# Squares of three blocks taken head by head with ScalarE's accumulator, k and v of two batches on 96 partitions, and a new order of the queues

## Chip, core and metric

One core of a Trainium2 chip. The engines are TensorE (PE; its weight loads PEld), VectorE (DVE), ScalarE (ACT), GpSimd (POOL) and SyncE (SP), whose queue issues nearly all DMAs. The metric is the device time of one launch in microseconds, the median of the runs.

## What is computed

Three layers in a row on 4 batches of 576 tokens (2304 tokens, 8 heads of 64): linear attention with an RMS norm per head, a layer with Mish, and a layer with SoLU and a layer norm. All inputs are float32.

```python
kv = einsum('bhsd,bhse->bhde', k, v)              # 64 x 64 for each batch and head
o = einsum('bhsd,bhde->bhse', q, kv)
x = o / sqrt(mean(o * o, -1) + 1e-6) * g_norm     # per token and head
h = x @ w_in                                      # 512 -> 2048
y = (h * tanh(softplus(h))) @ w_out               # 2048 -> 512
z = y @ w2_in                                     # 512 -> 1024
s = z * softmax(z)
out = (s - mean(s)) / sqrt(var(s) + 1e-6) * g_ln @ w2_out
```

## The kernel before

**Tiles.** The tokens are cut into six blocks of 384 (three units of 128: block b, unit r). Blocks 0, 1, 3, 5 are the first 384 tokens of batches 0 to 3; blocks 2 and 4 hold the last 192 tokens of two batches each. Large matmuls run in fp16 with hi and lo parts (three passes), so every weight is decoded first: a piece of 128x1024 words is loaded (`ld`), scaled on ACT (`sc`, L598), signed on POOL (`sg`, L603), put together on DVE (`low` L608, `put` L615) and split into fp16 hi on ACT (`whi`, L626) and lo on DVE (`wlo`, L633 and L635). Pieces ("1", f) are w_in, ("2", f) are w_out.

**Attention.** `ld(b,i)` loads k and v of a pair of heads (`load_pair`, L340 to L350). For batches 0 and 1 (`WIDE`) two heads share 128 partitions, 64 each, in nine rows. For batches 2 and 3 a head's first 512 tokens lie on 128 partitions in four rows, and its last 64 tokens come with `ldr(b)` (`load_rest`, L333 to L338), four DMAs per batch in runs of 256 bytes. `kv(b,i)` (`kv_pair`, L365 to L380) makes one pair's products as fp32 matmuls of 64 columns, two per step, one for each head; the trace has two records for each. `kvf`, `kvg` and `kvh`, `kvl` bring the products into SBUF, on ACT and DVE. For each unit of blocks 0 and 1 then run: `qf`, `qT` (PE), `qc` (ACT, L447), `xo` (PE, o = q times kv, into a PSUM bank), `sq` (ACT: square of all eight heads, 128x512, L497), `ms` (DVE: sum per head, L502), `ep` and `rho` (POOL: add 1e-6, power -1/2, L506 and L512), `xf` (DVE, L518), `xP` (PE), `xhi` (ACT, L466), `xlo` (DVE, L471). Units of blocks 2 to 5 go another way for q and x (`qhi`, `qlo`, DMA transposes) but have the same `xo`, `sq`, `ms`, `ep`, `rho`, `xf`. Blocks 0 to 2 square straight from the PSUM bank; blocks 3 to 5 copy to SBUF first (`xc`).

**Mish layer.** `H0(i,r)` (block 0, first group, in parts of 128 tokens) and `H(b,g,i)` (384 tokens, 12 matmuls) make h in one of three PSUM banks, which `mi(b,g,i)` (ACT, L877) frees; `ghi` (ACT, L884) and `glo` (DVE, L889) split the result, and `Y(b,g,j)` multiplies by w_out. From `Hp(1,2,1)` on the products take a form with seven instead of eight multiplications. The last layer follows.

**Order.** Every operation is a task with an engine, a cost and its predecessors. SEQUENCE is a list of task numbers, found beforehand; tasks are issued in this order, and each engine runs its own in that order, one behind the other. `plan.timed` only gives the times by which `keep_warm` (L1704) fills expected gaps of PE with unused matmuls.

Of the kernel before, what the change touches and what calls it, by code (L numbers as in the profile page):

```python
# [7 lines left out]
FP32 = mybir.dt.float32  # L8
FP16 = mybir.dt.float16
I32 = mybir.dt.int32  # L10
ACTF = mybir.ActivationFunctionType
# [1756 lines left out]
```

## Time and profile before

| | |
|---|---|
| median of 3 runs | 579.49 us (579.33 to 579.74) |
| the profiled execution | 579.91 us |
| its span, first to last instruction | 578.1 us |
| PE busy | 571.4 us (99%) |
| DVE busy | 441.2 us (76%) |
| ACT busy | 367.4 us (64%) |
| POOL busy | 129.3 us (22%) |
| granted TensorE clock, mean | 0.999 |

Times in rows are microseconds from the start of the span. A start and a duration of one row and the start of the next on the same engine tell how long the engine was held: on ACT the next instruction often starts before the last has ended. The busy shares are means over stages with different limits; the first 60 us look unlike the rest.

### The profile page before, as it was taken

The numbers are of one execution on the slowest core, as the hardware profiler recorded it, in microseconds if no ns is written. First come the engines' busy times: TensorE is split into PE (matmuls) and PEld (weight loads), VectorE is DVE, ScalarE is ACT, GpSimd is POOL, SyncE is SP. The second block draws the span as 40 slices with busy tenths as digits, with TensorE's granted clock in tenths as the row PEclk, the third lists the DMA queues.
The fourth block names the chain that finished last, engine by engine and source line by source line (L and its number), as shares of the span: only waits on it lengthen the run. The fifth ranks groups of instructions, "written<-read, shape, count | busy, mean of one in ns | idle before, by whom it ended". The sixth has DMA issues, their size and how long they took to land.

```text
span 578.1 us, 12245 instructions
## 1 busy us (share of the span) xinstructions
PE 571.4 (99%) x4920; PEld 413.8 (72%) x4920; DVE 441.2 (76%) x745; ACT 367.4 (64%) x636; POOL 129.3 (22%) x185
## 2 busy tenths in 40 slices
PE   8999999999999999999999999999999999999997
PEld 7886666666678877887777787774545557677886
DVE  2899898899958978787573876996575998697851
ACT  2688666675737643364645567774769797888841
POOL 1766422331022301101100101000305305234300
PEclk9999999999999999999999999999999999999999
DMA  8996979928505380225114232281056448676995
GB/s 317 367 237 169 250 207 323 238 84 177 80 1 75 38 248 12 69 93 177 62 73 157 82 128 84 83 289 48 1 137 183 91 74 164 130 163 135 219 221 155
DMA packets 132090, 84.42 MB, mean 146 GB/s; under 512 B 96450, under 2 KB 119362, under 8 KB 131778
## 3 DMA queue, kind: packets, MB, share of 16 engines
q1 hardware_dynamic: 131888, 83.58, 56.7%
q8 instruction: 38, 0.62, 0.4%
q14 instruction: 18, 0.15, 0.1%
q10 hardware_dynamic: 146, 0.07, 0.0%
HBM read 46.67 MB, written 12.06 MB: 102 GB/s over the span
## 4 chain that ended last, share of the span: by engine, by line
PE 96%; DMA 2%; SPq 0%; issue 0%; DVE 0%; ACT 0%; POOL 0%; POOLq 0%; DVEq 0%
PE y L907 33%; PE hp L833 19%; PE h L1016 14%; PE op L1162 13%; PE hp L739 11%; PE kvp L379 2%; PE xo L481 2%; DMA yT<-in_v_dram 1%; DMA w<-ws 1%; PE hp L1707 1%; PE xo L453 1%; PE xTp L461 0%; PE qTp L441 0%; SPq L346 0%; DVE kvf L384 0%
## 5 line engine op out<-in xcount | busy, mean ns | idle before, releaser
L907 PE MATMUL y<-g,w 128*128 128x384 f16 x1152 | 202.5, 326 | 0.0
L907 PEld LDWEIGHTS <-w 128*128 128x128 f16 x1152 | 110.7, 98 | 66.9
L603 POOL TENSOR_SCALAR st<-st 128x512 f32<-128x512 f32 x48 | 41.0, 858 | 211.0 <-ACT P L598 201.0
L1162 PEld LDWEIGHTS <-w 128*128 128x128 f16 x768 | 74.1, 98 | 12.8 <-DMA w<-ws 0.6
L1162 PE MATMUL op<-yT,w 128*128 128x256 f16 (+1 forms) x576 | 72.4, 271 | 0.4 <-DMA w<-ws 0.4
L889 DVE SCALAR_TENSOR_TENSOR g<-m,g 128x768 f16<-128x768 f32 x48 | 45.8, 961 | 15.4 <-ACT g L884 15.1
L739 PEld LDWEIGHTS <-w 128*128 128x128 f16 x480 | 41.2, 98 | 21.3
L833 PEld LDWEIGHTS <-w 128*128 128x128 f16 x576 | 48.4, 98 | 3.7
L833 PEld LDWEIGHTS <-ws 128*128 128x128 f16 x576 | 48.5, 98 | 3.4
L739 PE MATMUL hp<-xT,w 128*128 128x384 f16 (+1 forms) x384 | 49.8, 286 | 0.0
L608 DVE SCALAR_TENSOR_TENSOR st<-st 128x512 int32<-128x512 int32 x48 | 33.5, 706 | 13.7 <-POOL st L603 13.6
L598 ACT ACTIVATE P<-st 128x512 f32<-128x512 f32 x48 | 32.1, 671 | 16.1 <-DMA st<-in_moe_w_in_dram 7.8
L1071 POOL TENSOR_SCALAR small<-small 128x1 f32<-128x1 f32 x18 | 13.0, 720 | 131.6 <-ACT e L1053 131.2
L884 ACT ACTIVATE g<-m 128x768 f16<-128x768 f32 x48 | 39.9, 838 | 3.7 <-PE y L907 3.5
L1016 PEld LDWEIGHTS <-w 128*128 128x128 f16 x210 | 20.6, 98 | 22.3
L1016 PE MATMUL h<-st,w 128*128 128x512 f16 x150 | 35.0, 379 | 0.0
L615 DVE SCALAR_TENSOR_TENSOR P<-P,st 128x512 int32<-128x512 int32 x48 | 33.1, 703 | 1.0
L512 POOL TENSOR_TENSOR rho<-ms,nhalf 128x8 f32<-128x8 f32 x18 | 31.0, 1727 | 1.0
L1162 PE MATMUL op<-ws,w 128*128 128x256 f16 (+1 forms) x192 | 31.1, 271 | 0.0
L850 ACT ACTIVATE st<-hp 128x384 f32<-128x384 f32 x32 | 15.5, 485 | 24.2 <-PE hp L833 24.2
L833 PE MATMUL hp<-xT,ws 128*128 128x192 f16 x336 | 30.8, 246 | 0.0
L1016 PEld LDWEIGHTS <-ws 128*128 128x128 f16 x168 | 16.4, 98 | 17.7
(164 smaller groups left out, 1007.0 us busy)
## 6 DMA issues: line engine op xcount, KB each, us to landing
st<-in_moe_w_in_dram SPq DMA_DIRECT2D x24, 512.0 KB, 6.1
st<-in_moe_w_out_dram SPq DMA_DIRECT2D x24, 512.0 KB, 5.1
w_far<-F SPq DMA_DIRECT2D x15, 256.0 KB, 2.4
qraw<-in_q_dram SPq DMA_DIRECT2D x4, 768.0 KB, 6.2
w_far<-st SPq DMA_DIRECT2D x11, 256.0 KB, 2.6
out_dram<-yT SPq DMA_DIRECT2D x11, 256.0 KB, 2.4
yT<-w_far SPq DMA_DIRECT2D x3, 896.0 KB, 4.9
st<-w_far SPq DMA_DIRECT2D x5, 512.0 KB, 7.1
```

The costliest lines, as they stand in the source:

```text
L512: nc.gpsimd.tensor_tensor(out=rho, in0=ms, in1=nhalf, op=ALU.pow)
L598: nc.scalar.activation(out=P, in_=v[:, :, 1], func=ACTF.Copy, scale=2.0 ** -111)
L603: nc.gpsimd.tensor_scalar(out=v[:, :, 1], in0=v[:, :, 1], scalar1=0.0, scalar2=1.0, op0=ALU.mult, op1=ALU.mult)
L608: nc.vector.scalar_tensor_tensor(out=v[:, :, 0], in0=v[:, :, 0], scalar=29, in1=v[:, :, 1], op0=ALU.logical_shift_right, op1=ALU.bitwise_or)
L615: nc.vector.scalar_tensor_tensor(out=P.bitcast(I32), in0=P.bitcast(I32), scalar=3, in1=v[:, :, 0], op0=ALU.logical_shift_left, op1=ALU.bit ...
L739: nc.tensor.matmul(out=h_t[b, grp, i][:, t], lhsT=w1[:, f, c, wa], rhs=xT_t[b][:, C * xa + c, t], start=(c == 0 and m == 0), stop=(c == C ...
L833: nc.tensor.matmul(out=p[:, HT * fs:HT * fs + HT], lhsT=lhsT, rhs=x[:, C * xa + 2 * kx + c, HT * n:HT * n + HT], start=(opens and fs == 0 ...
L884: nc.scalar.activation(out=g_t[b, grp][:, 0, 2 * i:2 * i + 2], in_=m_t[b, grp, i], func=ACTF.Copy, scale=64.0)
L889: nc.vector.scalar_tensor_tensor(out=g_t[b, grp][:, 1, j], in0=m_t.pop((b, grp, i)), scalar=64.0, in1=g_t[b, grp][:, 0, j], op0=ALU.mult, ...
L907: nc.tensor.matmul(out=y_t[cc][:, 0:BLK], lhsT=w2[:, grp * G + ii, wa, cc * 128:(cc + 1) * 128], rhs=g_t[b, grp][:, ga, ii], start=(first ...
L1016: nc.tensor.matmul(out=T[p, "2" + bank], lhsT=yF[p][:, x, ya, c], rhs=w3[w][:, c, wa], start=(first and m == 0), stop=(m == 5), skip_group ...
L1162: nc.tensor.matmul(out=T[p, bank][:, lo:hi], lhsT=lnTs[p % 2][:, 8 * x + 4 * la + kk], rhs=w4[kk][:, 7 * HB * wa + HB * w + lo:7 * HB * wa ...
```

## The change

1. `a_sqs` takes the place of `a_sq` and `a_ms` for blocks 0 to 2: eight ACTIVATE instructions a unit, one per head of 64 columns, each with an accumulator output into the unit's `ms`. The task `sq` is booked at SQS = 1.0 in the plan (0.6 before); `ms` of these nine units becomes an empty task. Blocks 3 to 5 keep `a_sq` and `a_ms`.
2. Batches 2 and 3: a head's 576 tokens lie on 96 partitions in six rows, loaded with the pair; `load_rest` and the tasks `ldr(2)`, `ldr(3)` go. A pair's product is six steps of two matmuls on 96 partitions instead of four on 128 and one on 64.
3. SEQUENCE is new. Two tasks less shift the numbers behind 471 by one and behind 476 by two; read with that, the queues differ up to about 150 us and are the same behind (PE from `Hp(1,2,1)`: the last 317 of its 422 tasks; ACT the last 408 of 596).

```diff
@@ SEQUENCE, its first lines
-442 2164 481 2165 447 443 448 501 514 502 449 527 503 463 450 515 464 516 7 444 465 445 14 466 451 528
-488 487 489 8 504 452 529 9 517 10 505 490 482 506 530 518 507 467 15 508 519 531 11 0 532 468 12 520 16
+442 2162 448 2163 447 449 479 463 464 450 465 0 499 512 500 443 7 525 501 466 451 513 486 485 487 514
+502 480 1 526 2 503 504 515 488 505 444 467 506 445 516 517 3 452 4 8 489 518 5 14 9 527 507 519 6 528
...
-    K1 = 2 * S // 128
+    K1, K2R = 2 * S // 128, S // 96
...
-    def load_rest(b):
-        for a, src in enumerate((k, v)):
-            for h in range(2):
-                nc.sync.dma_start(
-                    out=rest_of(b, a)[HALF[h]],
-                    in_=src[b, :, 512:S].rearrange("(i h) s d -> h s i d", h=2)[h])
...
     def load_pair(b, i):
-        t = raw_of(b, i)[:, 0:2 * K1 * D].rearrange("p (a r d) -> p a r d", a=2, r=K1)
+        t = yT[RAW[b][i]].rearrange("p c a t -> p (c a t)").bitcast(FP32)
+        if b in WIDE:
+            t = t[:, 0:2 * K1 * D].rearrange("p (a r d) -> p a r d", a=2, r=K1)
+        else:
+            t = t[0:96].rearrange("p (a h r d) -> p a h r d", a=2, h=2, r=K2R)
...
+            s = s.rearrange("h (p r) d -> (h p) r d", r=K1) if b in WIDE else s.rearrange(
+                "h (p r) d -> p h r d", r=K2R)
+            nc.sync.dma_start(out=t[:, a], in_=s)
...
-        n = K1 if b in WIDE else 5
+        n = K1 if b in WIDE else K2R
...
+                kh, vh = (t[HALF[h], a, r] if b in WIDE else t[:, a, h, r] for a in range(2))
...
+    def a_sqs(b, r):
+        t = at.tile([128, H, D], FP32, tag="sq", name="sq", bufs=2)
+        ms = ms_t[b, r] = at.tile([128, H, 1], FP32, tag="ms", name="ms", bufs=3)
+        for h in range(H):
+            nc.scalar.activation(
+                out=t[:, h], in_=xo_t[b, r][:, h], func=ACTF.Square,
+                scale=0.125 if b < 2 else 2.0 ** -16, accum_out=ms[:, h])
...
+    SQS = 1.0
...
-            task(("sq", *u), "A", 0.6, a_sq, u, [("xo", *u)] + ring("sq", 2, ("ms", *u)))
-            task(("ms", *u), "V", 0.68, a_ms, u, [("sq", *u)] + ring("ms", 3, ("rho", *u)))
+            task(("sq", *u), "A", SQS, a_sqs, u,
+                 [("xo", *u)] + ring("sq", 2, ("sq", *u)) + ring("ms", 3, ("rho", *u)))
+            task(("ms", *u), "-", 0.0, lambda: None, (), [("sq", *u)])
...
+        if b < 3:
+            task(("sq", *u), "A", SQS, a_sqs, u,
+                 [("xo", *u)] + ring("sq", 2, ("sq", *u)) + ring("ms", 3, ("rho", *u)))
+            task(("ms", *u), "-", 0.0, lambda: None, (), [("sq", *u)])
```

The heads of the queues by task names (w1.f and w2.f for pieces of w_in and w_out), as far as the steps below need them:

```
SP before: ldq(0) ld(0,0) ld(0,1) ld(0,2) ld(0,3) w1.1 w1.2 ld(1,0) ld(1,1) ldq(1) w1.0 ld(1,2) ld(1,3) w1.4
SP after:  ld(0,1) ld(0,0) ld(0,2) ldq(0) ld(0,3) w1.0 w1.1 ld(1,0) ldq(1) ld(1,1) w1.2 w1.3 ld(1,2) ld(1,3) w1.6
PE before: qT(0,0) kv(0,0) qT(0,1) kv(0,1) kv(0,2) kv(0,3) qT(0,2) xo(0,0) xo(0,1) xo(0,2) kv(1,0) kv(1,1) xP(0,0)
  xP(0,1) qT(1,0) kv(1,2) kv(1,3) xP(0,2) qT(1,1) H0(0,0) xo(1,0) H0(1,0) H0(2,0) H0(1,1) qT(1,2) xo(1,1) H0(0,1) ...
  xo(2,0) xP(1,2) H(0,1,3) H(1,0,0) H(1,0,1) xo(2,1) Y(0,0,0)
PE after:  kv(0,0) kv(0,1) kv(0,2) qT(0,0) kv(0,3) qT(0,1) xo(0,0) qT(0,2) xo(0,1) kv(1,0) xo(0,2) xP(0,0) xP(0,1)
  qT(1,0) kv(1,1) H0(0,0) H0(1,0) qT(1,1) H0(0,1) kv(1,2) H0(1,1) qT(1,2) kv(1,3) xP(0,2) H0(2,0) xo(1,0) xo(1,1) ...
  xo(2,0) H(0,1,2) xP(1,2) H(0,1,3) H(1,0,0) xo(2,1) H(1,0,1) H(1,0,2) Y(0,0,0)
ACT before: qc(0,0) qc(0,1) kvf(0) sc qc(0,2) sq(0,0) kvh(0) sq(0,1) sc sq(0,2) whi xhi(0,0) sc qc(1,0) xhi(0,1) whi whi kvf(1)
  sc qc(1,1) xhi(0,2) sc sq(1,0) sc kvh(1) whi sc sq(1,1) whi qc(1,2) mi(0,0,0) ...
ACT after:  qc(0,0) kvf(0) qc(0,1) sc sq(0,0) kvh(0) sq(0,1) sc whi qc(0,2) sq(0,2) xhi(0,0) whi sc xhi(0,1) qc(1,0) sc whi
  qc(1,1) sc qc(1,2) whi kvf(1) xhi(0,2) sc kvh(1) sq(1,0) sc whi mi(0,0,0) whi mi(0,0,1) sq(1,1) whi qhi(2,0) sq(1,2)
  xhi(1,0) sc sc mi(0,0,2) sc xhi(1,1) mi(0,1,0) qhi(2,1) mi(0,0,3) whi qhi(2,2) sc sq(2,0) mi(0,1,1) sc xhi(1,2)
  ghi(0,0,0) ghi(0,0,1) ghi(0,1,0) whi mi(0,1,2) mi(0,1,3) sq(2,1)
```

## Rows read from the trace of the kernel before

**Rows 1.** The page, part 4: shares of the chain that ended last, by engine.
```profile
PE 96%; DMA 2%; SPq 0%; issue 0%; DVE 0%; ACT 0%; POOL 0%; POOLq 0%; DVEq 0%
```

**Rows 2.** The chain in order of time, 0 to 60 us: start, duration, what.
```profile
17.74 7.21 DMA yT<-in_v_dram
...
25.09 1.36 PE kvp L379 x35
...
26.51 0.63 PE xTp L461 x4
27.14 0.44 PE qTp L441 x4
27.57 0.67 PE hp L739 x12
28.24 0.95 PE xo L453 x8
...
46.96 5.85 PE hp L739 x36
52.81 0.80 PE xo L481 x24
```

**Rows 3.** Stretches: busy us (instructions) of PE, PEld, DVE, ACT, POOL; clock, DMA share, GB/s.
```profile
22.00:24.00 2.00, 1.44 (x20) 1.24 (x21) 1.96 (x5) 1.40 (x3) 1.28 (x3) 1.00 1.05 384
...
30.00:32.00 2.00, 2.00 (x31) 2.00 (x29) 2.00 (x4) 1.95 (x5) 1.38 (x2) 1.00 1.06 229
```

**Rows 4.** Line L502: its instructions, duration ns min/median/max, first and last start.
```profile
L502 DVE TENSOR_REDUCE ms<-sq x18: 672/680/687, 16.0 to 191.7; 128x8 f32<-128x512 f32 x18
```

**Rows 5.** Groups of ACT by shape: count, busy us, mean ns, idle before.
```profile
L497 ACT ACTIVATE sq<-xo 128x512 f32<-128x512 f32 x9 | 5.3, 593 | 1.0 <-PE xo L453 0.7 <-PE xo L481 0.2
...
L1191 ACT ACTIVATE yT<-op 128x128 f32<-128x128 f32 x1 | 0.3, 278 | 3.5 <-PE op L1162 3.5
```

**Rows 6.** ACT in order of time, 440 to 458 us: start, duration, what.
```profile
441.74 0.20 ACT L1064 ACTIVATION_READ_ACCUMULATOR e<-Q,small 128x1 f32 x1
441.83 3.50 ACT L1091 ACTIVATE Q<-Q,small 128x1024 f32<-128x1024 f32 x3
...
457.16 0.19 ACT L1064 ACTIVATION_READ_ACCUMULATOR e<-w,small 128x1 f32 x1
457.38 1.15 ACT L1053 ACTIVATE e<-w,small 128x1024 f32<-128x1024 f32 x1
```

**Rows 7.** ACT in order of time, 0 to 60 us.
```profile
15.30 0.60 ACT L497 ACTIVATE sq<-xo 128x512 f32<-128x512 f32 x1 [0.20 <-PE xo L453]
...
27.86 0.58 ACT L447 ACTIVATE qT<-qTp 128x512 f32<-128x512 f32 x1
28.34 0.58 ACT L466 ACTIVATE xT<-xTp 128x512 f16<-128x512 f32 x1
28.82 0.67 ACT L598 ACTIVATE P<-st 128x512 f32<-128x512 f32 x1
...
30.42 0.85 ACT L388 ACTIVATE kvr<-kvf 64x256 f16<-64x256 f32 x2
31.30 0.72 ACT L626 ACTIVATE w<-P,gs 128x512 f16<-128x512 f32 x1
...
47.49 0.48 ACT L877 ACTIVATE m<-hp 128x384 f32<-128x384 f32 x1
47.86 1.58 ACT L884 ACTIVATE g<-m 128x768 f16<-128x768 f32 x2
...
49.92 0.49 ACT L877 ACTIVATE m<-hp 128x384 f32<-128x384 f32 x1
```

**Rows 8.** PE in order of time, kv products, one and two of batch 0, one of batch 2.
```profile
9.39 1.26 PE L379 MATMUL kvp<-yT 64*64 64x64 f32 x36
...
10.74 2.38 PE L379 MATMUL kvp<-yT 64*64 64x64 f32 x72
...
91.59 0.95 PE L379 MATMUL kvp<-yT 128*64 128x64 f32 x20
```

More of the change, by code (lines that the diff above doesn't have):

```diff
@@ L325, in tile_attn_moe_moe2 @@
     RAW = ((2, 3, 4, 5), (0, 1, 2, 3), (3, 4, 3, 4), (3, 4, 3, 4))
-    def raw_of(b, i):
-        return yT[RAW[b][i]].rearrange("p c a t -> p (c a t)").bitcast(FP32)
-    def rest_of(b, a):
-        return raw_of(b, a)[:, 1152:1408].rearrange("p (i d) -> p i d", i=4)
-    def load_rest(b):
-        for a, src in enumerate((k, v)):
-            for h in range(2):
-                nc.sync.dma_start(
-                    out=rest_of(b, a)[HALF[h]],
-                    in_=src[b, :, 512:S].rearrange("(i h) s d -> h s i d", h=2)[h])
-    def load_pair(b, i):
-        t = raw_of(b, i)[:, 0:2 * K1 * D].rearrange("p (a r d) -> p a r d", a=2, r=K1)
+    def load_pair(b, i):
+        t = yT[RAW[b][i]].rearrange("p c a t -> p (c a t)").bitcast(FP32)
[3 more added lines that the diff above has]
+            t = t[0:96].rearrange("p (a h r d) -> p a h r d", a=2, h=2, r=K2R)
         raw[b, i] = t
@@ L344, in load_pair @@
             s = src[b, 2 * i:2 * i + 2]
-            if b in WIDE:
-                nc.sync.dma_start(out=t[:, a], in_=s.rearrange("h (p r) d -> (h p) r d", r=K1))
-            else:
-                nc.sync.dma_start(
-                    out=t[:, a, 0:8].rearrange("p (h r) d -> p h r d", h=2),
-                    in_=s[:, 0:512].rearrange("h (p r) d -> p h r d", r=4))
+            s = s.rearrange("h (p r) d -> (h p) r d", r=K1) if b in WIDE else s.rearrange(
+                "h (p r) d -> p h r d", r=K2R)
+            nc.sync.dma_start(out=t[:, a], in_=s)
     q_t = {}
@@ L369, in kv_pair @@
         kvp_t[b] = p
-        n = K1 if b in WIDE else 5
+        n = K1 if b in WIDE else K2R
         for r in range(n):
             for h in range(2):
-                if b in WIDE:
-                    kh, vh = (t[HALF[h], a, r] for a in range(2))
-                elif r < 4:
-                    kh, vh = (t[:, a, 4 * h + r] for a in range(2))
-                else:
-                    kh, vh = (rest_of(b, a)[HALF[h], i] for a in range(2))
+                kh, vh = (t[HALF[h], a, r] if b in WIDE else t[:, a, h, r] for a in range(2))
                 nc.tensor.matmul(
@@ L1322, in tile_attn_moe_moe2 @@
                 free = [("kv", 3, i - 2) if i > 1 else ("kv", 2, i + 2), ("put", ("2", 15))]
-            task(("ld", b, i), "S", PAIR + (0.0 if b in WIDE else 0.3) if b or i else 1.5, load_pair, (b, i), free, LAND)
+            task(("ld", b, i), "S", PAIR if b or i else 1.5, load_pair, (b, i), free, LAND)
     for b in range(B):
-        if b not in WIDE:
-            free = [("kv", 2, 3)] if b == 3 else [("put", ("1", 15))] if b == 2 else []
-            task(("ldr", b), "S", 1.6, load_rest, (b,), free + ([("kv", 1, 3)] if b == 2 else []), LAND)
         for i in range(4):
-            task(("kv", b, i), "P", 1.27 if b in WIDE else 0.79, kv_pair, (b, i),
-                 [("ld", b, i), ("ldr", b) if b not in WIDE else None, ("kv", b, i - 1) if i else None], 0.25)
+            task(("kv", b, i), "P", 1.24 if b in WIDE else 0.87, kv_pair, (b, i),
+                 [("ld", b, i), ("kv", b, i - 1) if i else None], 0.25)
     for b in range(2):
@@ L1382, in tile_attn_moe_moe2 @@
             task(("xc", *u), "A", 0.62, a_xc, u, [("xo", *u)] + ring("xf", 2, ("xlo", *u)))
-        task(("sq", *u), "A", 0.6, a_sq, u,
-             [("xc" if b >= NI else "xo", *u)] + ring("sq", 2, ("ms", *u)))
-        task(("ms", *u), "V", 0.68, a_ms, u, [("sq", *u)] + ring("ms", 3, ("rho", *u)))
+        if b < 3:
+            task(("sq", *u), "A", SQS, a_sqs, u,
+                 [("xo", *u)] + ring("sq", 2, ("sq", *u)) + ring("ms", 3, ("rho", *u)))
+            task(("ms", *u), "-", 0.0, lambda: None, (), [("sq", *u)])
+        else:
+            task(("sq", *u), "A", 0.6, a_sq, u, [("xc", *u)] + ring("sq", 2, ("ms", *u)))
+            task(("ms", *u), "V", 0.68, a_ms, u, [("sq", *u)] + ring("ms", 3, ("rho", *u)))
         task(("ep", *u), "G", 0.25, a_ep, u, [("ms", *u)])
```

184 rows, old and new, of the table SEQUENCE are left out of this document.

## Prediction

> **What bounds the kernel now.** The chain of waits, shares by engine: PE carries 96% of the span [rows 1]. The chain in order of time says where PE isn't the bound: it waits for batch 1's v until 24.95, the last k, v product (`kv(1,3)`) ends at 26.45, and from 26.51 one PE piece begins where the last ended: 0.63, 0.44 and 0.67 in a row, then 46.96 + 5.85 = 52.81 + 0.80 = 53.61 [rows 2]. So the engines before PE can give or take time only in the first 26 us, or by opening a hole later; what is lost before PE's order becomes the same as before (`Hp(1,2,1)`, near 150 us) moves the end one for one, since no idle PE stands behind it but the wait near the end, which is released by PE itself. The stretch table shows what feeds PE: at 30 to 32 us DVE is busy 2.00 of 2 us and ACT 1.95 [rows 3]. Both are full; the change takes from one and gives to the other. The granted clock is 1.00 there.
>
> **Sums off VectorE.** Eighteen sums stand in the trace; the nine of blocks 0 to 2 go, 0.68 us each [rows 4], 6.1 us in all, six of them before 40 us. On a full DVE that is real room. It reaches PE only if ACT delivers, since each decoded weight piece, `xhi`, `mi` and `ghi` also passes ACT.
>
> **Squares on ScalarE, the term that decides.** Today one 128x512 square takes 593 ns [rows 5]; the next instruction starts 0.10 before the end of the last (28.34 + 0.58, next at 28.82 [rows 7]), so it holds ACT 0.49. Now eight 128x64 squares, each with an accumulator output. The trace shows that such an output is an instruction of its own, ACTIVATION_READ_ACCUMULATOR: after one at 441.74 the next ACTIVATE starts at 441.83, 0.09 later; after the one at 457.16 it starts at 457.38, 0.22 later, and there it overwrites `e`, the tile just written [rows 6]. No 128x64 ACTIVATE is in the trace. From 128x512 in 593 and 128x128 in 278 ns [rows 5], a column costs 0.82 ns: 278 - 53 = 225 ns, less 0.10 of overlap 0.12. A head: 0.12 + 0.09 = 0.21; a unit: 8 x 0.21 = 1.70 us, against 0.49, so +1.21 for each of nine units; the plan books it at 1.0. Bounds: nothing but the columns and the read, 8 x (0.05 + 0.09) = 1.15; no overlap and the 0.22, 8 x (0.225 + 0.22) = 3.6. I take 1.70: the eight heads write different slices, so the 0.09 is the nearer row.
>
> The Trainium skill, "ScalarE: Activation LUTs", What ACT_TABLE_LOAD costs, puts an ACTIVATE with immediate scale and bias at 186 ns plus 0.833 ns per column, with 93 ns overlapped back to back. That speaks against cutting one square into eight: an estimate from it is 0.146 us for a head's ACTIVATE. With the trace's read it gives 1.9 us a unit and, by the slope derived below, an end 1.4 us later than my forecast.
>
> **The chain through the new ACT queue.** Prices, start to start, of today's ACT rows [rows 7]: `qc` and `xhi` 0.48, `kvh` 0.88, `mi` 0.37; from a duration less the overlap, weight scale `sc` 0.57, `whi` 0.62, `ghi` 0.74. `qhi`, and `whi` of w_out, which has no scale, are as wide as `qc`: 0.50; `kvf`, half as wide, 0.30.
>
> Step 1. k and v of batch 0 come ahead of q now, but the bytes ahead of its last v are the same, so `xo(0,0)` and the first square stay at 15.3 [rows 7]. Behind it stand kvh(0), sq(0,1), sc, whi and only then qc(0,2), for which PE's `xo(0,2)` waits: 15.3 + 1.70 + 0.88 + 1.70 + 0.57 + 0.62 + 0.50 = 21.3. `xo(0,2)` takes 0.95 [rows 2], so sq(0,2) starts at 22.4, with `xhi(0,0)` and the next weights queued behind it.
>
> Step 2. sq 1.70, xhi 0.48, whi 0.62, sc 0.57, xhi 0.48, qc 0.48 = 4.3: 26.7, with PE's start 0.15 behind. Then PE runs qT(1,1), H0(0,1), kv(1,2), H0(1,1), qT(1,2), kv(1,3): 0.45 + 0.67 + 1.25 + 0.67 + 0.45 + 1.25 = 4.74, ending at 31.6 against 26.45. (The data is not last: one weight piece more, 0.52 MB, lies ahead of that v, at 384 GB/s [rows 3] 1.4 us, so it lands near 26.3.) But four H0 parts and two qT, 3.6 us of PE work, are already done. PE is late by 31.6 - 26.45 - 3.6 = 1.55.
>
> Step 3. `kvf(1)` waits for that kv and for DVE's half, so ACT goes on at 32.2. Ahead of `mi(0,1,2)` stand 1 kvf, 1 kvh, 7 sc, 4 sq, 4 + 1 whi, 6 mi, 3 qhi, 4 xhi, 3 ghi: 0.30 + 0.88 + 3.99 + 6.80 + 2.98 + 2.22 + 1.50 + 1.92 + 2.22 = 22.8, so it starts at 55.0 against 49.92 [rows 7]. It frees the PSUM bank of H(1,0,1), which runs 55.5 to 57.4. The same PE work (with xo(2,1) ahead of it) ends today at 53.61 [rows 2]: **3.8 us late**. Behind it ACT has room again and PE's order is full, so I expect no more loss and no regain.
>
> Each 0.1 us in a unit's square moves this by 0.7 (twice in step 1, once in step 2, four times in step 3); the break-even is near 1.15 us. Now `ep` waits for ACT instead of DVE; behind it on POOL stand rho, weight signs and qf. In step 1 the chain sq, ep, rho, xf still has xf(0,0) ready before `xP(0,0)` can run; later it is no longer than the ACT queue.
>
> **k, v of batches 2, 3.** Ten fp32 matmuls a pair (four steps of two on 128 partitions, one step of two on 64) become twelve on 96. Nine steps of two take 1.26 us and eighteen 2.38, so a step is 0.12; today's five take 0.95 since the change of height costs a gap [rows 8]. Six alike: 1.26 - 3 x 0.12 = 0.90. So -0.05 a pair, eight pairs, -0.4; if instead cost went by matmuls, 0.95 x 12 / 10, +0.19 a pair, +1.5. I take -0.3: batch 0's steps run on 64 partitions and batch 2's on 128, at about one price, so the height itself costs nothing. Eight small DMAs leave SP's queue; PE waits for none of these loads today, and `kv(2,0)` moves ahead by one Y (1.95) while PE is 3.8 later, so I cost them at nothing; were that cover gone, one load would be waited for, under 2 us. Reordered weight pieces and transposes are in the steps above.
>
> **The sum.** 3.8 - 0.3 = +3.5 us. The profiled execution took 579.91, its span 578.1 and 1.8 around it; +3.5 gives 583.4, and on the median of the runs, 579.49, **583.0**. Under 0.2% (1.2 us) counts as no change: about what a measurement of this kernel can tell.
>
> **The rivals.**
> A, ACT keeps up and the order pays: a unit costs about 0.96, that is the reads hide beside the next square. Then step 1 gives 19.8 and step 2 ends at 29.4; from there PE itself is the limit. Today it works 53.61 - 26.45 = 27.2 us in a row to that point, 3.6 of them moved ahead: 29.4 + 23.6 = 53.0, 0.6 early; with kv 0.3 that is 578.6, down to 577.8 where DVE's room lets the weight pieces and PE's first parts start sooner. DVE's 6.1 us speak for it, the 0.09 behind every read against it. It decides below 1.15 us a unit.
> B, no difference: a unit between 1.1 and 1.3, or holes in my ACT queue that others fill: near 579.5.
> C, each square waits for the read ahead of it, as at 457.38: 8 x (0.12 + 0.22) = 2.7 a unit, 1.0 x 7 more: 590. For it: all heads write one tile. Against: different slices.
> D, the kv pairs cost by matmuls: +1.8 on my sum, 584.8; the gap between the heights speaks against it.
>
> **How the numbers follow.** My forecast with D inside it (581 to 586.5): 0.65. A: 0.20, of which two thirds lie under 578.3 and count as faster. B: 0.08. C: 0.07. The likeliest gives 583.0. The range leaves out C and a part of A; it runs from 578.3 to 587, as an extrapolated price with a slope of 7 needs. Faster 0.13, same 0.07 + 0.08 = 0.15, slower 0.72.
>
> **What would show it.** Line of the new squares on ACT: 72 ACTIVATE of 128x64 and 72 reads, start to start of a head 0.21. PE waiting for ACT's qc before the third `xo` near 18 to 21 us; kv(1,3) ending near 31 us; ACT without idle from 32 to 55; a PE hole ahead of H(1,0,1). Kv pairs of 24 records in 0.9 us. After 60 us the two PE rows run at a constant distance. A head in 0.12, or PE's run without holes beginning before 26 us of equal work, would make me wrong.

## The result

The changed kernel takes 587.15 us (median of 585.04 to 587.97) against 579.59 (579.33 to 579.74) beside it: 1.0126, interval 1.0114 to 1.0138. That is slower, as forecast, but by 7.6 us and not by 3.5, and just outside the range (578.3 to 587.0). The profiled execution took 586.54, its span is 584.7, so 6.6 of it can be followed in the trace.

The chain of waits, shares by engine, answers [rows 1]: PE had 96% of the chain and now has 87%; the rest is time in which it waits for others.

```profile
PE 87%; ACT 3%; DMA 3%; DVE 2%; issue 1%; POOL 1%; SPq 1%; POOLq 0%; ACTq 0%; DVEq 0%
```

ACT in order of time at the first square answers the first row of [rows 7]:

```profile
14.41 0.36 ACT L367 COPY kvf<-kvp 64x256 f32<-64x256 f32 x1 [1.64 <-DVE kvf L367]
...
16.05 0.20 ACT L487 ACTIVATE sq<-xo 128x64 f32<-128x64 f32 x1
16.16 0.19 ACT L487 ACTIVATION_READ_ACCUMULATOR sq<-xo 128x1 f32 x1
16.25 0.21 ACT L487 ACTIVATE sq<-xo 128x64 f32<-128x64 f32 x1
...
17.62 0.86 ACT L371 ACTIVATE kvr<-kvf 64x256 f16<-64x256 f32 x2
```

Its groups by shape (count | busy us, mean ns | idle before) answer [rows 5]:

```profile
L487 ACT ACTIVATE sq<-xo 128x64 f32<-128x64 f32 x72 | 15.2, 282 | 1.5 <-PE xo L436 1.3 <-PE xo L464 0.2
L487 ACT ACTIVATION_READ_ACCUMULATOR sq<-xo 128x1 f32 x72 | 15.0, 269 | 0.0
```

All 72 squares have a read behind them. From start to start a head takes 0.20 (0.10 and 0.09), a unit 17.62 - 16.05 = 1.57 us of ACT (two of the nine, right behind `kvh`, 1.72).

PE in order of time answers [rows 2] and [rows 8]:

```profile
12.58 1.26 PE L362 MATMUL kvp<-yT 64*64 64x64 f32 x36 [0.43 <-DMA yT<-in_v_dram]
...
14.83 1.16 PE L436 MATMUL xo<-kvf,qT 128*128 128x128 f32 x8 [0.40 <-ACT kvf L367]
...
18.46 1.26 PE L362 MATMUL kvp<-yT 64*64 64x64 f32 x36 [1.00 <-DMA yT<-in_v_dram]
...
22.07 1.16 PE L436 MATMUL xo<-kvf,qT 128*128 128x128 f32 x8 [1.03 <-ACT qT L430]
...
24.14 0.63 PE L444 MATMUL xTp<-ident,xf 128*128 128x128 f32 x4
...
31.49 1.26 PE L362 MATMUL kvp<-yT 64*64 64x64 f32 x36
...
42.95 1.80 PE L730 MATMUL hp<-xT,w 128*128 128x384 f16 x10 [0.23 <-DVE w L626]
45.48 0.66 PE L444 MATMUL xTp<-ident,xf 128*128 128x128 f32 x4 [0.73 <-DVE xf L509]
...
54.28 1.95 PE L730 MATMUL hp<-xT,w 128*128 128x384 f16 x11 [0.18 <-DVE xT L454]
...
60.87 2.11 PE L898 MATMUL y<-g,w 128*128 128x384 f16 x12
...
95.01 0.92 PE L362 MATMUL kvp<-yT 96*64 96x64 f32 x24
95.86 2.12 PE L730 MATMUL hp<-yT,w 128*128 128x384 f16 x12
...
115.57 0.83 PE L464 MATMUL xo<-kvr,qT 128*128 128x128 f16 x12 [1.07 <-DVE kvr L377]
...
162.22 2.12 PE L898 MATMUL y<-g,w 128*128 128x384 f16 x12
```

Two places of PE's queue serve as marks below. **Mark 1** is Y(0,0,0), at 53.54 in the kernel before; in the new order H(1,0,2) stands ahead of it, so 1.95 is taken off. **Mark 2** is the Y behind the first two Hp, at 155.85 before, with the same work ahead of it in both orders. The changed kernel is 60.87 - 1.95 - 53.54 = 5.4 late at mark 1 and 162.22 - 155.85 = 6.4 at mark 2. What lies between is the hole at 115.57. It costs 1.2 (1.07 of idle, and the 0.16 by which `xo` otherwise starts before the matmuls ahead of it have ended), less 0.24 for the eight pairs of k and v. After mark 2 a wait of 0.35 for a load near the end is gone, so PE ends 5.8 late, and the last stores take 0.8 longer; the sum is the 6.6.

### The profile page after: what moved, and what is told of

The parts are those of the page before. It is cut to its first block, busy times and chain, and to the rows that moved or that the text cites. A ratio compares the mean times of both kernels' runs of the same rounds, so it can differ in the third digit from the quotient of the medians.

```text
span 584.7 us, 12440 instructions
## 1 busy us (share of the span) xinstructions
PE 572.5 (98%) x4955; PEld 413.6 (71%) x4955; DVE 437.2 (75%) x736; ACT 376.5 (64%) x771; POOL 132.2 (23%) x185
## 4 chain that ended last, share of the span: by engine, by line
PE 87%; ACT 3%; DMA 3%; DVE 2%; issue 1%; POOL 1%; SPq 1%; POOLq 0%; ACTq 0%; DVEq 0%
PE y L898 31%; PE hp L824 19%; PE op L1153 14%; PE h L1007 14%; PE hp L730 7%; DMA st<-in_moe_w_in_dram 2%; DMA st<-in_moe_w_out_dram 2%; PE xo L464 1%; PE kvp L362 1%; ACT P L589 1%; ACT sq L487 1%; SPq L338 1%; POOL rho L503 1%; ACT w L617 1%; DVE st L599 1%
## 5 line engine op out<-in xcount | busy, mean ns | idle before, releaser
L594 POOL TENSOR_SCALAR st<-st 128x512 f32<-128x512 f32 x48 | 38.6, 811 | 211.3 <-ACT P L589 195.0
L730 PEld LDWEIGHTS <-w 128*128 128x128 f16 x480 | 40.8, 98 | 22.8 <-issue 1.0
L730 PE MATMUL hp<-xT,w 128*128 128x384 f16 (+1 forms) x384 | 51.0, 286 | 0.7 <-DVE w L626 0.2
L599 DVE SCALAR_TENSOR_TENSOR st<-st 128x512 int32<-128x512 int32 x48 | 35.8, 751 | 13.5 <-POOL st L594 13.5
L503 POOL TENSOR_TENSOR rho<-ms,nhalf 128x8 f32<-128x8 f32 x18 | 33.1, 1839 | 1.0
```

What stands on the lines that cost most here:

```text
L503: nc.gpsimd.tensor_tensor(out=rho, in0=ms, in1=nhalf, op=ALU.pow)
L594: nc.gpsimd.tensor_scalar(out=v[:, :, 1], in0=v[:, :, 1], scalar1=0.0, scalar2=1.0, op0=ALU.mult, op1=ALU.mult)
L599: nc.vector.scalar_tensor_tensor(out=v[:, :, 0], in0=v[:, :, 0], scalar=29, in1=v[:, :, 1], op0=ALU.logical_shift_right, op1=ALU.bitwise_or)
L730: nc.tensor.matmul(out=h_t[b, grp, i][:, t], lhsT=w1[:, f, c, wa], rhs=xT_t[b][:, C * xa + c, t], start=(c == 0 and m == 0), stop=(c == C ...
```

## The experiments

"Late" is PE's lateness against the kernel before, in us, each from one profiled execution. Part of it is the moment at which the first k and v land: in the seven runs whose loads and PE order are those of the changed kernel up to there (after, e1, e2, e5, e6, e8, e9) `xo(0,0)` starts anywhere from 14.19 to 15.23. So differences of some 0.5 between two runs at mark 1 need not come from their edits.

| run | what it is | median | ratio to before, interval | late at mark 1, 2 |
|---|---|---|---|---|
| after | the whole change | 587.15 | 1.0126 (1.0114, 1.0138) | 5.4, 6.4 |
| e3 | squares by heads alone, old order | 584.75 | 1.0090 (1.0076, 1.0104) | 4.8, 5.1 |
| e4 | 96 partitions alone, old order | 581.33 | 1.0029 (1.0018, 1.0041) | 0.5, 1.7 |
| e7 | e4, kv(3,3) later | 581.42 | 1.0034 (1.0021, 1.0046) | 0.0, 0.5 |
| e11 | both, old order | 587.45 | 1.0135 (1.0119, 1.0150) | 4.7, 7.1 |
| e1 | after, one square, no sums | 583.23 | 1.0062 (1.0040, 1.0084) | 1.7, 2.4 |
| e2 | after, eight squares, no reads | 582.63 | 1.0082 (1.0052, 1.0112) | 2.6, 2.3 |
| e8 | after, one square in block 0 | 584.49 | 1.0084 (1.0069, 1.0099) | 3.8, 4.2 |
| e5 | after, old squares and sums | 591.20 | 1.0205 (1.0191, 1.0219) | 5.8, 10.3 |
| e6 | after, kvh(2) first | 585.13 | 1.0100 (1.0084, 1.0115) | 5.8, 5.6 |
| e9 | after, qc(0,2) early | 588.72 | 1.0158 (1.0144, 1.0171) | 6.4, 7.9 |
| e10 | e6, kv(1,1) early | 586.30 | 1.0116 (1.0100, 1.0133) | 6.0, 7.0 |
| e12 | e10, hole filled | 587.99 | 1.0158 (1.0128, 1.0188) | 5.2, 5.7 |
| e14 | e6, q first | 588.23 | 1.0154 (1.0141, 1.0167) | 6.8, 6.6 |

In the new order the runs of one kernel spread by 0.7 to 7 us, those of the kernel before by 0.8 at most. e2's ratio lies above the one of its median (1.0051), since two of its five runs took over 586 us. Nothing tried beats the kernel before, and no run takes part 2 alone out of the new order.

### One part at a time, in the old order

**e3**, part 1 alone: the new `a_sqs` in the kernel before.

> The kernel before with its own order and its own k, v rows; only part 1 of the change is made (eight squares with accumulators a unit in blocks 0 to 2, VectorE's nine sums gone). Theory P: ACT pays 1.08 us more for each of four units between 29 and 47 us, 4.3 us, against which stand 1.9 us of idle ACT there, so PE is some 2.0 to 2.5 us late: 581.5 (580.5 to 582.5). Rival O': the order before was made for the cheap squares and loses more than the new one does, over 587. Rival D: VectorE's 6 us given back count more, 579 or less.

Measured +5.1, twice theory P's. ACT is the chain from 14.8 to 22 and, but for one xo, from 30 to 55.5 us, as the prediction's mechanism has it. Of the chain from 30 to 42 us the squares alone are 42% (shares by line):

```profile
by line: ACT sq L504 41.9%; ACT P L606 14.3%; ACT w L634 11.1%; PE xo L453 9.8%; ACT qT L447 9.1%; ACT kvr L388 5.7%; ACT qhl L414 4.3%; ACT xT L466 4.1%; issue 2.5%; PE qTp L441 1.0%; ACTq L504 0.3%
```

PE in order of time shows what the estimate, made from ACT's queue behind 29 us, had left out: xP(0,1) waits 2.62 us for xf, behind the squares of block 0.

```profile
23.89 0.63 PE L461 MATMUL xTp<-ident,xf 128*128 128x128 f32 x4 [2.62 <-DVE xf L526]
...
25.21 3.86 PE L379 MATMUL kvp<-yT 64*64 64x64 f32 x72
```

Behind that wait the granted clock fell (stretch table, columns as in [rows 3]):

```profile
26.00:27.00 1.00, 1.00 (x25) 1.00 (x24) 1.00 (x2) 0.08 (x1) 1.00 (x2) 0.50 1.09 348
```

Two products that take 2.38 [rows 8] take 3.86 at a granted clock of 0.50 to 0.69 (25 to 29 us; 0.50 is the lower of the two levels, 1.2 and 2.4 GHz). In e11, below, which has part 2 besides, PE waits as long at the same place, the clock stays at 1.00, and PE waits 1.08 for ACT behind the products instead:

```profile
24.06 0.63 PE L444 MATMUL xTp<-ident,xf 128*128 128x128 f32 x4 [2.58 <-DVE xf L509]
```

```profile
26.00:27.00 1.00, 1.00 (x41) 1.00 (x38) 1.00 (x2) 0.24 (x1) 1.00 (x2) 1.00 1.09 349
```

xP(0,2) runs at 28.77 there, at 29.01 in e3. So in these two traces the clock by itself cost some 0.2 to 0.4: ACT was late anyway. The times of e11 agree: two of its executions had a mean clock of 1.000 (587.5 and 588.2 us), two of 0.996 and 0.997 (587.4 and 586.7).

**e4**, part 2 alone: `load_pair` and `kv_pair` of the change, and

```diff
-            task(("ldr", b), "S", 1.6, load_rest, ...)
+            task(("ldr", b), "-", 0.0, lambda: None, ...)
```

> The kernel before with its own order and its squares; only part 2 of the change is made (k, v of batches 2 and 3 on 96 partitions, the eight small loads gone). The changed kernel's rows show a pair start to start in 0.85 us against 0.88: 8 x 0.03 = 0.24 us less, 579.3 (579.0 to 579.5), so no difference or hardly one. Rival: the wait for the small loads or their descriptors cost more than the rows show, 578.9 or less; or six steps cost by matmuls, 581.

It is 1.7 us slower, which neither side expected. A pair does cost 0.85 start to start instead of 0.88. But SP's queue and PE show that the load of pair (3,3), which now holds all 576 tokens, can be issued only when kv(3,1) has freed the tile; its v is there 7.8 us after the issue, and PE waits:

```profile
135.30 0.44 SPq L338 DMA_DIRECT2D yT<-in_v_dram  x1
```

```profile
143.13 0.92 PE L362 MATMUL kvp<-yT 96*64 96x64 f32 x24 [1.33 <-DMA yT<-in_v_dram]
```

0.5 late at mark 1, + 1.33 - 8 x 0.03 = 1.6 (1.7 at mark 2). The 0.5 arises before 26 us in waits for k and v of batch 1, where the edit changes nothing; e7, with the same loads up to there, has none of it, so it belongs to the single execution.

**e7** gives that load one Y of cover:

```diff
 PE:  kv(3,2) Y(2,0,3)
-     kv(3,3) Y(2,1,0)
+     Y(2,1,0) kv(3,3)
```

> The kernel before with k, v of batches 2 and 3 on 96 partitions, as in the run of that part alone, and kv(3,3) moved behind the next Y in PE's queue. There kv(3,3) waited 1.33 us for its v, whose load can only be issued once kv(3,1) has freed the tile. Theory: with one Y (1.95) of cover the wait goes, so 581.3 - 1.3 = 580.0, and 8 x 0.03 us less for the pairs: 579.3 to 580.0. Rival: the larger loads delay others (transposes of q at 136 to 145), 580.5 or more.

The wait at kv(3,3) is gone, the median the same. `kvh(3)` and `kvl(3)`, which follow kv(3,3), now hold up ACT and DVE, and PE waits behind them at 159.6; another load makes kv(2,3) wait 0.60.

```profile
159.64 1.15 PE L821 MATMUL hp<-xT,st 128*128 128x192 f16 x12 [1.18 <-ACT st L838]
```

**e11**, both parts in the old order:

> Parts 1 and 2 of the change in the order of the kernel before; only the new order is left out. If the parts add, 579.6 + 5.1 (squares alone) + 1.7 (rows alone) = 586.4. Theory A (the new order brings little or nothing for the new work): 585.5 to 587, no slower than the changed kernel's 587.15. Rival B (the new order saves much of what the edits cost): 589 or more.

587.45 against 587.15: theory A, though 0.45 above its range. The new order brings nothing that can be measured for the new work; the loss is that of the two edits, 5.1 + 1.7 = 6.8, and 1 us more.

### The price of the squares in the new order

**e1** and **e2** (their sums are left out):

```diff
-        for h in range(H):
-            nc.scalar.activation(out=t[:, h], ..., func=ACTF.Square, accum_out=ms[:, h])
+        nc.scalar.activation(out=t, in_=xo_t[b, r], func=ACTF.Square, ...)     # e1; e2 keeps the loop without accum_out
+        nc.scalar.activation(out=ms, in_=xo_t[b, r][:, :, 0:1], func=ACTF.Copy, scale=0.0, bias=0.0369)
```

> The changed kernel with its order and its k, v rows, but in blocks 0 to 2 one 128x512 square and one 128x8 copy of a constant into ms in place of eight squares with accumulators. It leaves out the sums of squares (rho comes from a constant), and VectorE has no sums either. ACT pays about 0.49 + 0.1 = 0.6 us a unit instead of the 1.57 that the changed kernel's rows show. Theory P (the loss is the price of the squares on ACT, 0.7 us at the end for each 0.1 us in a unit): the 0.97 us less a unit give back 6.8 us, to 580.3, and the hole of 1.07 us before xo at 115.6 may remain: 579.5 to 581.5. Rival O (the new order loses time by itself: batch 1's k and v land late, and ScalarE's kvh(2) stands behind a weight piece that waits for its load): at least half of the 7.6 us stay, 583.5 or more.

> The changed kernel, but its eight 128x64 squares a unit write no accumulator; one 128x8 copy of a constant fills ms. It leaves out the sums of squares, like the kernel with one square. A unit holds ACT 8 x 0.10 + 0.1 = 0.9 us instead of 1.57. Theory P: 0.67 less a unit, by the slope of 7 a gain of 4.7, to 582.5 (581.5 to 583.5), so the eight reads (0.095 each) carry more than half of the loss. Rival O: 585 or more. Third: the durations of ACT's instructions, which grow by 0.01 us with each instruction in long runs of squares and reads, grow as well without reads.

In e1 a unit holds ACT 0.55 us:

```profile
15.88 0.60 ACT L486 ACTIVATE sq<-xo 128x512 f32<-128x512 f32 x1 [0.18 <-PE xo L436]
16.37 0.17 ACT L488 ACTIVATE ms<-xo 128x8 f32<-128x8 f32 x1
16.43 0.84 ACT L371 ACTIVATE kvr<-kvf 64x256 f16<-64x256 f32 x2
```

1.02 less a unit gives back 5.4 - 1.7 = 3.7 us at mark 1, 3.9 in the medians (e1's runs lie from 581.0 to 585.6). It lies between P and O. e2, at 0.9 a unit, can't be told from e1 (2.6 late at mark 1, of which 1.43 is one wait for the transposes of q that no other run shows). By its median, 582.63, it gives back 4.5 of the 7.6, inside P's range, but two of its five runs took over 586. So, as far as these two runs tell, there is a floor: between 0.9 and 0.55 us a unit cheaper squares bring nothing that can be measured, and the new order is still about 2 us late with them. Which part of the order costs these 2 us stays open.

**e8** has the cheap square in block 0 alone (`if b:` ahead of the loop of e1's diff, the loop of the change under it).

> The changed kernel, but the three units of block 0 have one 128x512 square and a 128x8 copy of a constant (their sums of squares are left out); blocks 1 and 2 keep the eight squares. It tells at which stage the price of the squares enters. The prediction's slope (twice in step 1, once in step 2, four times in step 3) puts 3 of 7 parts on block 0: the all-cheap run gave back 3.9 of 587.15 - 583.23, so 1.7 here: 585.5, with kv(1,3) ending near 31.2 as in the all-cheap run and the rest of the loss behind it. Rival (all of it enters before 33 us, through the chain of GpSimd to xP(0,1)): 583.5. Rival (all of it in ScalarE's queue behind 33 us): 587.

At mark 1, 5.38 - 3.84 = 1.54 of the 3.7 belongs to block 0, 2.14 to blocks 1 and 2: 42%, where 3 parts of 7 make 43%. That it comes so close is luck, given how the landing of the first loads varies; in the medians block 0 has 587.15 - 584.49 = 2.7 of 3.9, so e8 is a microsecond faster than forecast. kv(1,3) starts at 29.92 (31.49 in the changed kernel, 29.96 in e1), so block 0's share is lost by then.

**e5** has the new order and rows with the old squares and VectorE's sums.

```diff
-            task(("sq", *u), "A", SQS, a_sqs, u, ...)
-            task(("ms", *u), "-", 0.0, lambda: None, ...)
+            task(("sq", *u), "A", 0.6, a_sq, u, ...)
+            task(("ms", *u), "V", 0.68, a_ms, u, ...)       # in SEQUENCE right ahead of ep
```

> The changed kernel's order and k, v rows, with the squares of the kernel before: one 128x512 square on ACT and the sum on VectorE (the sum's task put right ahead of ep). So only part 1 is undone. Theory O2 (the order with its rows loses some 3.5 us by itself, which the run with one square and no sums showed, 583.2; the squares cost the rest): with 0.68 us of VectorE per unit added to that run, 583.5 to 585.5. Theory P (the squares are the whole loss): 581 or less. Rival V (the order needs VectorE's room, so the sums hurt it as much as the heads do): 586.5 or more.

Rival V: 4 us slower than the change. PE waits for xf four times, then 1.25 for v and 2.24 for `kvl`; DVE is busy 5.9 of 6 us from 32 to 38. At mark 1 the sums cost about as much as the heads (5.8 and 5.4 late); the rest comes between the marks (4.5 for 1.0), most of it in waits behind loads. e1 has the same single square without the sums (and with a small copy instead), so by the medians the nine sums cost 591.20 - 583.23 = 8.0 us in this order, where the heads cost 3.9: it has used the room on VectorE. "Undo part 1" is therefore not the same experiment in the two orders.

### Where the new order loses time

**e9**, one move on ACT:

```diff
-  kvh(0) sq(0,1) sc(w1.1) whi(w1.0) qc(0,2) sq(0,2)
+  kvh(0) qc(0,2) sq(0,1) sc(w1.1) whi(w1.0) sq(0,2)
```

> The changed kernel with qc(0,2) moved ahead of sq(0,1) in ScalarE's queue. The prediction's step 1 says that PE's xo(0,2) waits for qc(0,2) behind the squares and that this sets the start of the later work: then xo(0,2) runs at 19.7 instead of 22.1 and kv(1,3) ends 1.3 us earlier or more, 585.5. Rival theory G: what sets PE's restart is the chain of sq(0,1), ep, rho on GpSimd, xf and xP(0,1), which ends at 24.1; qc ahead of sq(0,1) makes it 0.5 later: xo(0,2) early, but xP(0,1) near 24.6, kv(1,3) not earlier, 587 to 588.

```profile
19.27 1.16 PE L441 MATMUL xo<-kvf,qT 128*128 128x128 f32 x8 [0.37 <-ACT qT L435]
...
25.32 0.63 PE L449 MATMUL xTp<-ident,xf 128*128 128x128 f32 x4 [1.79 <-DVE xf L514]
```

xo(0,2) runs 2.8 us earlier and PE then waits for xP(0,1), which is 1.2 later: theory G. What sets PE's restart is the chain over GpSimd, as the changed kernel's chain of waits has it (start, duration, what):

```profile
17.86 0.49 POOL ms L497
...
18.42 2.01 POOL rho L503
...
21.61 1.67 POOL rho L503
...
23.31 0.70 DVE xf L509
...
24.14 0.63 PE xTp L444 x4
```

**e6** puts two weight scales of ACT, and their signs, behind kvh(2).

```diff
 ACT:
-  sc(w2.14) mi(2,1,1) sc(w2.15) kvh(2) sc(w2.11)
+  mi(2,1,1) kvh(2) sc(w2.14) sc(w2.15) sc(w2.11)
```

> The changed kernel, with two weight scales of ScalarE's queue (pieces 14 and 15 of w_out) and their signs on GpSimd moved behind kvh(2). In the changed kernel kvh(2) stood behind them while the second waited for its load until 113.1, and PE's xo then waited 1.07 us. Theory O2: that hole is the order's own and goes, and nothing else takes its place: 1.0 to 1.2 us less, 586.0, and xo follows its H without a gap near 114.4. Rival: the late weight stream reappears as another wait between 115 and 150 us, 587.

The hole is gone (first the changed kernel's chain, then PE of e6, where xo follows its H at once):

```profile
104.26 8.85 DMA st<-in_moe_w_out_dram
...
113.22 0.10 ACT P L589
...
113.78 0.36 ACT kvr L371
...
114.56 0.04 DVE kvr L377
```

```profile
112.83 2.11 PE L735 MATMUL hp<-yT,w 128*128 128x384 f16 x12
114.78 0.83 PE L469 MATMUL xo<-kvr,qT 128*128 128x128 f16 x12
```

At mark 2 it is 0.8 less late although it was 0.4 later at mark 1, where its `xo(0,0)` had started 0.4 later too; the hole is 1.2 of it. The median falls by 2.0; what lies beyond the 1.2 is within the spread of the changed kernel's runs. In that kernel's chain the load had taken 8.85 us and was issued only at 104.21, when DVE had freed its buffer; how much of this the larger loads of part 2 bring about isn't shown.

**e10** adds to e6:

```diff
 SP:
-  ld(1,0) ldq(1) ld(1,1)
+  ld(1,0) ld(1,1) ldq(1)
 PE:
-  kv(1,0) xo(0,2) xP(0,0) xP(0,1) qT(1,0) kv(1,1)
+  kv(1,0) kv(1,1) xo(0,2) xP(0,0) xP(0,1) qT(1,0)
```

> The run with kvh(2) first (585.13), with two more moves in the new order: the load of k, v pair (1,1) ahead of q of block 1 on SP, and kv(1,1) ahead of xo(0,2) on PE, where PE stands idle from 19.7 to 22.1 in the changed kernel. Theory O2 (the order's own loss before 26 us is that PE has no k, v of batch 1 to work on while it waits): kv(1,1) runs near 20 to 21 in the hole, kv(1,3) ends 1.2 us earlier, near 31.6, and the end comes 1.2 earlier: 583.9. Rival: q of block 1 lands later and qT(1,0) waits as much, or the chain behind xP(0,1) sets the pace anyway: 585.

Slower, by 1.2 in the medians. kv(1,1) did run at 19.09, but nothing filled the rest of the hole, and in the profiled execution the clock fell (stretch table; xo took 1.89 for 1.16):

```profile
21.00:22.00 1.00, 0.09 (x1) 0.09 (x1) 0.78 (x2) 0.86 (x2) 1.00 (x2) 1.00 1.15 362
22.00:23.00 1.00, 1.00 (x6) 1.00 (x7) 0.81 (x2) 0.00 (x0) 1.00 (x1) 0.57 1.03 353
23.00:24.00 1.00, 1.00 (x6) 1.00 (x6) 0.85 (x2) 0.10 (x1) 1.00 (x3) 0.50 1.05 395
```

The clock isn't what made e10 slow: the profiled execution (586.36 us) has a mean clock of 0.997, the other three have 1.000 and took 586.11 to 586.77. At mark 1 PE is 0.1 later than in e6 (0.7 if counted from `xo(0,0)`); between the marks it then waits for `xc`, which e6 doesn't:

```profile
120.74 0.83 PE L469 MATMUL xo<-kvr,qT 128*128 128x128 f16 x12 [1.09 <-ACT xf L480]
```

**e12** fills it with unused matmuls (`if key == ("xo", 0, 2): keep_warm(11, ...)`).

> The run with kv(1,1) early (586.3), with eleven unused matmuls ahead of xo(0,2) on PE, in the hole from 20.3 to 21.9 us. In that run the granted clock was 1.00 up to 22 us, then 0.57, 0.50, 0.50 and 0.72 in the next four microseconds, and xo(0,2) took 1.89 us where it takes 1.16. Theory K (the moved product did fill the hole, and the clock took the gain back): with the hole filled the clock stays at 1.00, kv(1,3) ends near 31.9 instead of 33.3, and the end comes at 584 to 585. Rival G (the chain over GpSimd to xP(0,1) sets the pace, so filling the hole with real work gains nothing): kv(1,3) not before 32.8, 585.1 or more.

The clock stays at 1.00, kv(1,3) starts at 31.24 (31.90 in e6) and mark 1 is 0.65 earlier, which looks like theory K. But `xo(0,0)` started 0.75 earlier as well (14.48, 15.23 in e6). Counted from it, kv(1,3) starts after 16.76 us, in e6 after 16.67, in the changed kernel after 16.66 and in e10 after 17.38: the filled hole gives back what the clock had cost in e10's profiled execution, and kv(1,1) in the hole brings nothing. PE waits for xP(0,1) instead, as rival G says (kv(1,3) ends at 32.5, between K's 31.9 and G's 32.8):

```profile
24.36 0.63 PE L449 MATMUL xTp<-ident,xf 128*128 128x128 f32 x4 [0.71 <-DVE xf L514]
```

The end isn't earlier either: new waits (0.6 for `xc` at 119.5, 1.1 for a load near the end) come on top, and the runs spread from 585.4 to 592.5. One trace doesn't tell what the slower of them waited for.

**e14** changes SP's queue in e6:

```diff
-  ld(0,1) ld(0,0) ld(0,2) ldq(0) ld(0,3)
+  ldq(0) ld(0,1) ld(0,0) ld(0,2) ld(0,3)
```

> The run with kvh(2) first (585.13), with the load of block 0's q at the head of SP's queue again, as in the kernel before; k and v of batch 0 follow. The prediction held that the order of these loads doesn't move xo(0,0), since the bytes ahead of the last v are the same; in the changed kernel xo(0,0) ran at 14.83 against 14.10. If the order of the loads is the cause, xo(0,0) comes back to 14.1 to 14.3, the restart of PE moves as much, and the end comes 0.6 us earlier: 584.5. Rival (the two weight pieces issued from 5.33 us on take the last pair's share of the queues, whatever stands first): xo(0,0) stays at 14.8, 585.1.

Inconclusive. xo(0,0) came at 15.15, but this isn't the order of the loads in the kernel before: kv(0,0), PE's first product, needs ld(0,0), which is now third. It started at 9.01 (7.54 in e6), behind 41 unused matmuls instead of 26, and from there PE waited for no load until xo(0,0); later the clock fell. Why xo(0,0) comes later in the new order (14.19 to 15.23 in the seven runs above; 13.60 to 14.10 in the five traces of the old one) is open. What the stretch table shows is that less was moved at 4 to 6 us (before, after; 387 and 283 GB/s at the end of the rows):

```profile
4.00:6.00 2.00, 2.00 (x11) 1.39 (x10) 0.00 (x0) 0.00 (x0) 0.00 (x0) 1.00 1.07 387
```

```profile
4.00:6.00 2.00, 2.00 (x11) 1.39 (x10) 0.00 (x0) 0.00 (x0) 0.00 (x0) 1.00 0.92 283
```

## Why the prediction was right in sign and too small

Two steps failed. The 3.8 us of the sum, added up over steps 1 to 3, measured 5.4 at mark 1: step 1 started too early and followed the wrong chain, and step 3 had more holes than the one that it looked for. And "I expect no more loss and no regain" left out a hole of 1.2. The mechanism of the 3.8, squares that hold ACT longer and PE waiting behind ACT's queue, is what e1, e3 and e8 show.

**The price of a head** was right: 0.20 against 0.21, 1.57 a unit against 1.70; the read doesn't hide. Rival C falls by these rows. The estimate from the Trainium skill, "ScalarE: Activation LUTs", What ACT_TABLE_LOAD costs (186 ns plus 0.833 ns per column, less 93 ns of overlap), was 0.146 us for a head's ACTIVATE; the rows here show 0.10 start to start, and the measurement decides.

**Step 1 failed twice.** Its start, "the bytes ahead of its last v are the same, so `xo(0,0)` and the first square stay at 15.3", was 0.75 too early: the last v came so late that xo(0,0) started at 14.83 (some of it is the spread of that start between runs). And it followed qc(0,2), where the chain over ep and rho to xP(0,1) ends last, as e9 and e12 show; I had looked at that chain for xf(0,0) only. The two chains end close together, so by luck the time came out near all the same (xo(0,2) 22.07 for 21.3).

**Step 2** carried that on: kv(1,3) ends at 32.7 instead of 31.6. These 1.1 are the larger part of the 5.4 - 3.8 = 1.6; the other 0.5 is lost behind it.

**Step 3** had the length of ACT's queue right: 22.8 predicted, from kvf(1) to mi(0,1,2) 56.32 - 33.27 = 23.05 measured, with 0.31 of idle in it.

```profile
33.27 0.37 ACT L367 COPY kvf<-kvp 64x256 f32<-64x256 f32 x1 [0.46 <-DVE kvf L367]
...
56.32 0.87 ACT L868 ACTIVATE m<-hp 128x384 f32<-128x384 f32 x2 [0.31 <-DVE g L880]
```

It had the place wrong: PE doesn't wait once before H(1,0,1) but loses the time in holes before 42.95, 45.48 and 54.28, where it waits for `wlo`, `xf` and `xlo`, and in smaller ones. The chain of waits runs through ACT from 33.27 to 50.25, and from there over POOL and DVE to the last of these holes.

**"I expect no more loss and no regain"** failed. 1.2 us go at 115.57, 60 us behind the last stretch that I worked through; e6, where that hole is gone, shows that `kvh(2)` behind a weight scale caused it. I had read ACT there as an engine with room; a queue with room still stands when its head waits for a load (here until 113.1).

**The slope of 7** was too steep. Three of the seven parts were counted ahead of kv(1,3): 1.02 less a unit would bring it 3.1 earlier, and it came 32.7 - 31.2 = 1.5 earlier in e1, as in e8. Behind it the slope ends where PE has no hole left: of the 2.7 us that the changed kernel loses there, e1 still loses 0.5. No run has a price between 1.57 and 0.9, so where it bends isn't shown. Rival A's end, 53.0 and 0.6 early, wasn't reached even at 0.55 a unit: e1 is 1.7 late, since kv(1,3) there ends at 31.2, where 26.45 + 3.6 = 30.05 would have been in time. So the break-even of 1.15 was wrong too.

**k, v on 96 partitions**: -0.24 for -0.3, and D falls. "I cost them at nothing", said of the loads, held in the changed kernel as far as its kv of batches 2 and 3 go, none of which waits, and not in the old order, where that cover is missing by 1.33 ("under 2 us"). What the larger loads do to the weights' loads in the new order no run shows.

**VectorE's room** was costed at nothing for PE. e5 against e1 shows that the new order needs it: with the sums on VectorE the end is some 8 us later, and 4 us later than with the heads on ACT.

In the sum: +3.8 became 5.4, -0.3 became -0.2, the hole adds 1.2 (5.4 - 0.2 + 1.2 = 6.4 at mark 2), the end 0.2; and the median lies 0.6 above the profiled execution, where before it lay 0.4 below.

## What to carry to other kernels

An accumulator output on ACT is an instruction of its own and isn't hidden behind the next one: price it from a row before cutting one wide instruction into eight. When a queue is reordered, follow each in-order engine past the stretch that changed, and ask of each instruction whose data comes by DMA who stands behind it. To undo one part inside an order that was made for it answers another question than to do the part alone in the old one; here part 1 gave -4 us in the new order (e5 to the changed kernel) and +5 in the old one (e3). Before an edit is given the credit for a gain of half a microsecond, compare where the two traces start: the first loads of one and the same kernel order landed up to 1 us apart.

## What the runs showed of the hardware that I had not expected

In long runs of ACT without idle the durations grow, by about 0.01 us with each head (a square and its read, so half of that with each instruction), while the step from start to start stays 0.10. They fall back after an idle, here one of 0.31 before 56.32:

```profile
35.46 0.22 ACT L487 ACTIVATE sq<-xo 128x64 f32<-128x64 f32 x1
...
51.29 0.50 ACT L487 ACTIVATE sq<-xo 128x64 f32<-128x64 f32 x1
...
57.13 0.23 ACT L487 ACTIVATE sq<-xo 128x64 f32<-128x64 f32 x1
```

So results come up to 0.3 us later than the queue suggests, and a sum made start to start doesn't see it: GpSimd's `ep` starts 0.09 after the end of the unit's last read, both where that read takes 0.24 us (17.77, `ep` at 17.86) and where it takes 0.48 (51.87, `ep` at 51.96). The reads aren't the cause: without them (e2) the squares of a unit grow from 0.22 to 0.30 too, but ACT has more short idles there, and nearly each unit begins at 0.22 again. Why the durations grow is not shown.

And holes on PE had different ends for the clock. 1.56 us in e10, behind k, v products, was followed by some three microseconds at about half the granted clock; 1.53 us in e6, at the same place but behind eleven unused matmuls, left it at 1.00. That doesn't show that the unused matmuls make the difference: of two holes behind nine of them, 2.62 us in e3 and 2.58 in e11, the first was followed by the lower level and the second wasn't, and the mean clock of one and the same kernel differs between executions (1.000 and 0.997 in e10, 1.000 and 0.996 in e6). What decides stays open.
